# A transformer block on one core: 512-token chunks, contraction tiles of 128 and 64 rows, a clock warm-up and a planned order

## The chip, the cores and the metric

The kernel runs on one core of one Trainium2 chip. The metric is the device time of one execution in microseconds (us). An execution is called slow when it lies over 1.5% above the fastest of the same kernel; only fast runs are compared. TensorE (PE in the profile) does the matmuls, VectorE (DVE), ScalarE (ACT) and GpSimd (POOL) the rest, and SyncE (SP) issues the transfers.

## The reference

2048 tokens of width 448, 16 heads of 28, hidden width 1792; everything is bfloat16.

```python
mod = silu(c) @ w_mod                       # six vectors of 448: sa, ca, ga, sb, cb, gb
h = layernorm(x) * (1 + ca) + sa
q, k, v = split(h @ wqkv)                   # 16 heads of 28
# each token attends to itself and to the 7 tokens before it at distances 2, 4, ... 14
x = x + ga * (softmax(q k / sqrt(28)) v) @ wo
h = layernorm(x) * (1 + cb) + sb
x = x + gb * (silu(h @ w1) @ w2)
```

Since the window steps by 2, even and odd tokens ("parities") never meet in attention. Both kernels treat them as two sequences of 1024 and cut each into 9 blocks of 114 queries, each with 128 keys.

## The kernel before

The width 448 is contracted as 4 tiles of 112 rows. The parts that matter:

```python
KT, KP = 4, 112
x_view = A_x...rearrange("(a p two) d -> two a p d", two=2, p=128)   # one token per row: 896 bytes

def transposes(ts, ...):                    # one token tile: 4 transposes, 112 columns apart
    for j, t in enumerate(ts):
        for k in range(KT):
            T.transpose(ps[:, k, c0:c0 + 128], t[:, KP * k:KP * k + 128], ident[:])

def mod_cols(vecs, dst0):                   # modulation vectors as columns: 64 matmuls of one column in all
    for i, v in enumerate(vecs):
        for j in range(KT):
            for k in range(KT):
                T.matmul(ps[0:m, i, j:j + 1], lhsT=wmod[:, k, ...], rhs=scT[:, k:k + 1], ...)

def wo_unit(a):                             # output projection
    for kk in range(KT):
        T.matmul(ps[:, 0:D], lhsT=oT[par][:, kk, ...], rhs=wo[:, kk, :], ...)

# first FFN product: 1024 tokens of a parity as 384 + 384 + 256 columns
T.matmul(ps[:, j, 0:n], lhsT=w1[:, kk, ...], rhs=h2T[k % 2][:, kk, 0:n], ...)
# ... six groups of blocks; attention of group k+1 is woven with the FFN of group k, in program order
```

## Time and profile before

| | before |
|---|---|
| median time (first three runs) | 216.81 us (216.11 to 219.19) |
| profiled run, its span | 220.84 us, 219.0 us |
| mean granted clock of TensorE, profiled run | 0.953 |
| the same in most fast runs | 0.97 |

The profiled run is 0.8 to 2.2% slower than the three others, at a lower clock than fast runs. Its parts and waits can be read, but its span is some 0.017 x 219 = 4 us too long (an estimate from the two clocks).

TensorE's "busy" time overstates its work, because the ends of pipelined matmuls are modelled. For this document I therefore sum **occupancy**: from the start of each matmul to the start of the next, less the idle time that the trace marks between them, added up by the tile that is written. "At full clock" means the mean of those issued while the granted clock was 1.0, times their number. What the occupancy has above that I call the half-clock excess. These sums are worked out from the records of the traces and stand in no view as they are.

### The profile page before, as it was taken

To read this page: it belongs to the slowest core of one execution; us is meant where nothing else is said; L and a number is where in the kernel's file an instruction comes from. 1 tells how busy PE (TensorE), PEld (TensorE's weight loads), DVE (VectorE), ACT (ScalarE), POOL (GpSimd) and SP (SyncE) were. 2 spreads that over 40 slices of the span, in tenths; PEclk is the share of its full clock that TensorE was granted. 3 is DMA by queue.
4 is the path that set the end of the run, shared out by engine and by line. 5 is a ranking of instruction groups with operands and counts; after the bars stand their busy time and mean duration, and the time that the engine had idled before them with its cause. 6 is when DMAs were issued, how large, how long until landed. Compare 5 with 4: busy or idle time off the path is not lost.

```text
span 219.0 us, 4124 instructions
## 1 busy us (share of the span) xinstructions
PE 194.5 (89%) x1739; PEld 118.0 (54%) x1739; DVE 122.7 (56%) x274; ACT 102.2 (47%) x133; POOL 17.3 (8%) x55
## 2 busy tenths in 40 slices
PE   0157999499968999999999999999999999999990
PEld 0143556237735456554665546866475546555840
DVE  4176386927899355755453186773887457642011
ACT  3004449254172656474425767428753735430610
POOL 2802004000021000010001000001000100010000
PEclk9999999757995999999999999999999999999996
DMA  5999999300000000001000001000000010001001
GB/s 153 267 229 227 220 221 229 115 0 0 3 0 3 0 1 3 0 0 45 21 3 0 0 24 43 3 0 0 24 21 3 0 44 22 0 4 42 21 27 28
DMA packets 9072, 11.22 MB, mean 51 GB/s; under 512 B 472, under 2 KB 8152, under 8 KB 9048
## 3 DMA queue, kind: packets, MB, share of 16 engines
q1 hardware_dynamic: 9040, 10.90, 21.0%
q8 instruction: 15, 0.25, 0.5%
q14 instruction: 9, 0.07, 0.1%
q10 hardware_dynamic: 8, 0.00, 0.0%
HBM read 9.06 MB, written 1.84 MB: 50 GB/s over the span
## 4 chain that ended last, share of the span: by engine, by line
PE 75%; DMA 9%; DVE 7%; SPq 4%; POOL 2%; issue 1%
PE ps_h L395 22%; PE ps_y L411 20%; PE ps_qk L235 9%; DMA x_all<-in_A_x_dram 9%; PE ps_v L243 6%; PE ps_wo L350 5%; PE ps_l L265 4%; PE ps_o L330 3%; PE ps_t L195 3%; DVE st L174 2%; PE ps_ot L343 2%; POOL rs L177 1%; SPq L108 1%; DVE xn L449 1%; SPq L98 1%; DVE qk L237 1%
## 5 line engine op out<-in xcount | busy, mean ns | idle before, releaser
L395 PE MATMUL ps_h<-h2T,w 112*128 112x384 bf16 (+1 forms) x336 | 53.9, 308 | 0.0
L396 ACT ACTIVATE hid<-ps_h 128x768 bf16<-128x768 f32 (+1 forms) x42 | 31.0, 739 | 41.5 <-PE ps_h L395 41.4
L411 PE MATMUL ps_y<-w,hid 128*128 128x448 bf16 x224 | 46.3, 353 | 0.0
L395 PEld LDWEIGHTS <-w 112*128 112x128 bf16 x336 | 32.2, 98 | 15.8
L267 ACT ACTIVATE p<-ps_l 128x912 bf16<-128x912 f32 (+1 forms) x36 | 33.1, 934 | 15.5 <-PE ps_l L265 15.4
L235 PE MATMUL ps_qk<-h1T,wp 112*128 112x456 bf16 (+2 forms) x192 | 36.6, 340 | 1.1 <-DVE h1T L206 0.7
L411 PEld LDWEIGHTS <-hid 128*128 128x128 bf16 x224 | 20.1, 98 | 18.2
L302 DVE TENSOR_TENSOR p<-p,maskb 128x1824 bf16<-128x1824 bf16 (+1 forms) x18 | 19.8, 1103 | 13.6 <-ACT p L267 13.6
L235 PEld LDWEIGHTS <-wp 112*128 112x128 bf16 x192 | 19.2, 105 | 12.8 <-issue 6.1
L174 DVE BATCH_NORM_STATS2 st<-x_all 128x6 f32<-128x448 bf16 x32 | 19.2, 614 | 3.8 <-DMA x_all<-in_A_x_dram 3.4
L415 DVE TENSOR_TENSOR ot<-ps_y,x_all 128x448 bf16<-128x448 f32 x16 | 9.9, 622 | 19.5 <-PE ps_y L411 19.5
L243 PE MATMUL ps_v<-wqkv,h1T 112*128 112x448 bf16 x72 | 17.7, 389 | 0.0
L265 PE MATMUL ps_l<-qk 28*128 28x114 bf16 (+1 forms) x288 | 14.3, 219 | 3.6 <-DVE qk L237 2.8
L176 POOL TENSOR_TENSOR rs<-mv,epsb 128x2 f32<-128x2 f32 (+2 forms) x11 | 3.2, 293 | 173.6 <-DVE mv L175 173.6
L265 PEld LDWEIGHTS <-qk 28*128 28x128 bf16 x288 | 8.3, 96 | 16.0 <-issue 15.5
L206 DVE TENSOR_SCALAR h2T<-ps_t,modc 112x384 bf16<-112x384 bf16 (+1 forms) x24 | 9.4, 448 | 11.8 <-PE ps_t L195 11.8
L351 DVE TENSOR_TENSOR x_all<-ps_wo,x_all 128x448 bf16<-128x448 f32 x16 | 10.0, 624 | 10.2 <-PE ps_wo L350 10.2
L204 ACT ACTIVATE h1T<-ps_t,modc 112x512 bf16<-112x512 bf16 (+1 forms) x10 | 6.3, 688 | 20.0 <-DVE h1T L206 20.0
L245 ACT CAST v<-ps_v 128x448 bf16<-128x448 f32 x18 | 8.8, 535 | 14.6 <-PE ps_v L243 14.4
L195 PE MATMUL ps_t<-ident,xn 128*128 128x128 bf16 x128 | 12.2, 251 | 3.7 <-DVE xn L185 2.5
L350 PE MATMUL ps_wo<-wo,oT 112*128 112x448 bf16 x64 | 14.6, 353 | 0.0
L237 ACT CAST qk<-ps_qk 128x912 bf16<-128x912 f32 (+2 forms) x12 | 8.8, 731 | 10.5 <-PE ps_qk L235 10.5
(63 smaller groups left out, 155.7 us busy)
## 6 DMA issues: line engine op xcount, KB each, us to landing
w<-in_B_w_dram SPq DMA_DIRECT2D x2, 1568.0 KB, 23.3
out_dram<-ot SPq DMA_DIRECT2D x16, 112.0 KB, 1.7
wmod<-in_w_mod_dram SPq DMA_DIRECT2D x1, 1568.0 KB, 19.2
x_all<-in_A_x_dram SPq DMA_DIRECT2D x3, 448.0 KB, 18.3
wqkv<-in_A_wqkv_dram SPq DMA_DIRECT2D x3, 392.0 KB, 10.8
wmod<-in_w_mod_dram SPq DMA_DIRECT2D x1, 784.0 KB, 8.4
x_all<-in_A_x_dram SPq DMA_DIRECT2D x2, 224.0 KB, 2.9
wo<-in_A_wo_dram SPq DMA_DIRECT2D x1, 392.0 KB
```

The lines of the kernel that those rows point to most:

```text
L174: V.bn_stats(out=st[:, j, :], in_=x_all[:, u, :])
L195: T.transpose(ps[:, k, c0:c0 + 128], t[:, KP * k:KP * k + 128], ident[:])
L235: T.matmul(ps[:, j, 0:n], lhsT=wp[:, k, 16 * typ + 4 * g:16 * typ + 4 * g + 4, :].rearrange("p h d -> p (h d)"), rhs=h1T[par][:, k, HALO + ...
L237: (S.copy if on_act else V.tensor_copy)(out=dst, in_=ps[:, :, 0:n])
L243: T.matmul(ps[:, j, 0:D], lhsT=h1T[par][:, k, BQ * b + 2:BQ * b + 130], rhs=wqkv[:, k, 2 * D:3 * D], start=(k == 0), stop=(k == KT - 1))
L265: T.matmul(ps[:, j, g * nq:(g + 1) * nq], lhsT=qk[par][r:r + DH, 4 + g, BQ * b + 2:BQ * b + 130], rhs=qk[par][r:r + DH, g, HALO + BQ * b:H ...
L267: S.activation(out=pbuf(par, b)[:, t, :, :, 0:nq], in_=ps[:, :, 0:4 * nq].rearrange("p j (g q) -> p j g q", q=nq), func=ACTF.Exp, scale=SCALE)
L302: V.tensor_tensor(out=p, in0=p, in1=maskb[:, 1 if b == 0 else 0, 0:nq].unsqueeze(1).to_broadcast([128, H, nq]), op=ALU.mult)
L350: T.matmul(ps[:, 0:D], lhsT=oT[par][:, kk, 128 * a:128 * a + 128], rhs=wo[:, kk, :], start=(kk == 0), stop=(kk == KT - 1))
L395: T.matmul(ps[:, j, 0:n], lhsT=w1[:, kk, 128 * f:128 * f + 128], rhs=h2T[k % 2][:, kk, 0:n], start=(kk == 0), stop=(kk == KT - 1))
L396: S.activation(out=hid[k % 2][:, 2 * i:2 * i + 2, 0:n], in_=ps[:, :, 0:n], func=ACTF.Silu)
L411: T.matmul(ps[:, 0:D], lhsT=hid[k % 2][:, f, 128 * j:128 * j + 128], rhs=w2[:, f, :], start=(f == 0), stop=(f == NF - 1))
```

## The change

The intent: wider matmuls (512 columns instead of 342 to 456), loads with longer rows on all 128 partitions, a warm TensorE clock at the first projection, no table switches between exponential and Silu, and no holes, by running all attention ahead of the FFN in an order that a list scheduler plans on the host. The diff, cut to its core:

```diff
-KT, KP = 4, 112
+KT, K3 = 4, D - 384                        # contraction 448 = 3 x 128 + 64
+NC, CP = 4, 256                            # 4 chunks of 512 consecutive tokens: 256 of each parity
+WARM, LA = 26, 3                           # LA: how many chunks attention runs ahead of the FFN
+def half(j):
+    return slice(K3 * j, K3 * j + K3)      # rows 0 to 63 or 64 to 127
+def rows_of(k, j=0):
+    return half(j) if k == 3 else slice(0, 128)

-x_view = ...rearrange("(a p two) d -> two a p d", two=2, p=128)
+x_view = ...rearrange("(c i p t) d -> c p i (t d)", c=NC, i=2, t=2)    # two tokens per row: 1792 bytes

 # transposes of a token tile, for both norms (and the same five for the attention output)
-    for k in range(KT):
-        T.transpose(ps[:, k, c0:c0 + 128], t[:, KP * k:KP * k + 128], ident[:])
+    for k in range(3):
+        T.transpose(ps[:, k, ...], x[:, 128 * k:128 * k + 128], ident[:])
+    for h in range(2):                     # the last 64 columns go to both halves of the rows
+        T.transpose(ps[half(h), 3, ...], x[:, 384:D], ident[:])

 # modulation columns
-        T.matmul(ps[0:m, i, j:j + 1], lhsT=wmod[:, k, ...], rhs=scT[:, k:k + 1], ...)
+        for h in range(1 + (j == 3)):
+            T.matmul(ps[rows_of(j, h), i, j:j + 1], lhsT=wmod[rows_of(k), k, ...], rhs=scT[rows_of(k), k:k + 1], ...)

 # output projection
-    T.matmul(ps[:, 0:D], lhsT=oT[par][:, kk, ...], rhs=wo[:, kk, :], ...)
+    T.matmul(ps[:, 0:D], lhsT=oT[rows_of(kk), kk, par, ...], rhs=wo[rows_of(kk), kk, :], ...)

 # Q, K and the first FFN product, in pairs of pairs: 6 full, 4 half, 6 full matmuls of 512 columns
+def duo(mms, ...):
+    for j in range(2):
+        for k in range(3):
+            mms[0](p0, j, k, k == 0, False)
+    for j in range(2):
+        mms[0](p0, j, 3, False, True)      # 64 rows each: product j on half j of the array
+    for j in range(2):
+        mms[1](p1, j, 3, True, False)
+    for j in range(2):
+        for k in range(3):
+            mms[1](p1, j, k, False, k == 2)

+def warm_up(o):                            # 27 times, while the weights load
+    T.matmul(warm[0][:, 0, :], lhsT=ident[:], rhs=ident[:].unsqueeze(1).to_broadcast([128, 4, 128]), ...)

-weave(...)                                 # hand-made order
+class Plan: ...                            # list scheduler with a cost in ns for every operation, for example
+    P.op(("pe", 280.0), tr, ...)           #   five norm transposes
+    P.op(("pe", 250.0), tr, ...)           #   five transposes of the attention output
+    P.op(("pe", 756.0), wo_mm, ...)        #   output projection of one token tile
```

## The prediction

> **What bounds the kernel now.** I read the page's busy line first, then the busy time by stretches, then TensorE's waits, then the chain in order of time. The page:
>
> ```profile
> PE 194.5 (89%) x1739; PEld 118.0 (54%) x1739; DVE 122.7 (56%) x274; ACT 102.2 (47%) x133; POOL 17.3 (8%) x55
> ```
>
> TensorE leads, but busy is not useful here. I cut the span where its behaviour changes (columns: busy us and instruction count of each engine, granted clock, DMA share, GB/s):
>
> ```profile
> 0.00:16.16 16.16, 3.68 (x49) 3.35 (x50) 7.02 (x35) 2.01 (x4) 6.65 (x37) 1.00 0.91 216
> 16.16:24.30 8.14, 6.98 (x29) 3.35 (x29) 5.04 (x15) 2.73 (x6) 1.20 (x2) 1.00 1.05 221
> 24.30:39.30 15.00, 15.00 (x136) 8.46 (x135) 9.26 (x27) 10.53 (x15) 2.42 (x4) 1.00 1.08 234
> 39.30:42.10 2.80, 0.01 (x1) 0.03 (x1) 2.80 (x4) 0.00 (x0) 0.00 (x0) 0.90 0.32 102
> 42.10:51.70 9.60, 9.56 (x55) 4.18 (x55) 3.99 (x4) 5.59 (x8) 0.00 (x0) 0.50 0.01 2
> 51.70:75.00 23.30, 20.67 (x242) 13.84 (x240) 18.92 (x42) 9.73 (x14) 2.12 (x2) 0.85 0.01 1
> 75.00:213.60 138.60, 138.58 (x1233) 84.75 (x1231) 75.04 (x150) 71.60 (x89) 4.91 (x10) 1.00 0.04 14
> 213.60:219.00 5.40, 0.00 (x0) 0.00 (x0) 0.62 (x1) 0.00 (x0) 0.00 (x0) 0.68 0.10 29
> ```
>
> From 75 us on TensorE is never free and never slowed, and VectorE and ScalarE are half idle: that stage is bound by TensorE. Before 75 us it is idle for 19.1 us (12.5 of them before its first projection at 16.16) and slow twice at a granted clock near one half. There is a third slow stretch that the clock column hides: between 18.2 and 24.3 us the weight loads of the 456-column projections follow each other at 0.38 us, which is 456 columns at 1.2 per ns, half pace; after 24.3 us at 0.19. What TensorE waited for, and what its groups cost once warm (waits; then pieces of the chain: start, us, matmuls):
>
> ```profile
> PE ps_m L215 <- DMA wmod<-in_w_mod_dram: 7.0, 1, 7.0
> PE ps_l L265 <- DVE qk L237: 2.8, 1, 2.8
> PE ps_t L195 <- DVE xn L185: 2.5, 2, 1.7
> ```
> ```profile
> 75.80 1.65 PE ps_qk L235 x8
> 77.45 1.51 PE ps_v L243 x8
> 80.89 1.30 PE ps_h L395 x8
> 88.26 0.76 PE ps_wo L350 x4
> 208.29 5.31 PE ps_y L411 x28
> ```
>
> The first wait is the start (weights not there), the second is the hole at 39 to 42 us after which the clock drops. Eight 384-column matmuls take 1.30 us, 162 ns each; 448 columns take 189 ns.
>
> **What the Trainium skill says.** (1) "TensorE: Matmul & The Clock Gate", Part 1: the array starts at 1.2 GHz, is released to 2.4 after a busy window of about 3.4 us and throttled after an idle one. The trace agrees on the halving (0.50 from 42.1 to 51.7) but the fall follows a hole of 2.8 us and the return took over 9 us of busy work, so recovery costs more here than the page's window. (2) Same page, "Back-to-back issue gap": N/2.4 + 2.5 ns. Agrees: 160 + 2.5 for 384 columns. (3) Same page, Part 3: matmuls in different row groups run at once. The logits of before use row groups of 32: eight 114-column matmuls, 50 ns each alone, take 0.30 us from their start to the next group's (75.43 to 75.73 in the timeline), so 0.75 of the serial time and not half. (4) "DMA: Bandwidth & Descriptors", Measured: 341 GB/s for a transfer of 1 MB. The loads of before reach it only at the end:
>
> ```profile
> 9.00:15.00 6.00, 3.01 (x46) 2.93 (x47) 2.92 (x11) 0.00 (x0) 2.28 (x17) 1.00 1.13 227
> 27.00:34.00 7.00, 7.00 (x78) 4.02 (x75) 5.36 (x12) 3.66 (x6) 0.99 (x2) 1.00 1.04 214
> 37.00:39.00 2.00, 2.00 (x22) 1.20 (x19) 0.60 (x3) 1.76 (x2) 1.21 (x2) 1.00 1.09 307
> ```
>
> At 27 to 34 us the first FFN weight moves with rows of 3584 bytes on 112 partitions, at 37 to 39 the second with rows of 896 bytes on 128. So long rows alone don't speed a load in this trace; filling 128 partitions may.
>
> **The change, part by part.**
> *Contraction 448 as 3 x 128 + 64 instead of 4 x 112.* The 64-row remainders of two products sit on two halves of the array, so eight passes become six full and two half ones. With the 0.75 from the logits a pair of 512-column outputs costs 6 x 0.216 + 2 x 0.75 x 0.216 = 1.62 us. First FFN product: 28 x 1.62 = 45.4 us, against 224 x 0.1625 + 112 x 0.109 = 48.6. Q and K: 16 x 1.62 = 25.9 against 27.8. V: 9 x (6 + 1.5) x 0.189 = 12.8 against 13.6. Together 5.9 less. Wider matmuls as such give only 2.5 ns for each one saved, already in these sums. Unchanged: second FFN product 224 x 0.190 = 42.5, output projection 64 x 0.19 = 12.1, logits 36 x 0.30 = 10.7, attention times V 18 x 0.405 = 7.3. Dearer: five transposes instead of four for each token tile, 9.0 against 7.9 for the norms and 4.5 against 3.7 for attention; modulation columns 80 x 36 ns = 2.9 against 2.35. Gates 1.5. Sum: **174.6 us of TensorE work, against some 180** before (138.6 after 75 us, 41.6 before it).
> *Clock warm-up.* 27 dummy matmuls of 512 columns in the time when TensorE waits for weights anyway. They cost nothing and can save the half-speed stretch 16.2 to 24.3: 6.98 busy at half pace, 3.5 us.
> *Start.* The first projection needs tokens (0.46 MB), modulation weights (0.80) and now the whole QKV weight (1.20): 2.46 MB; before, 2.06 without V. In before the QK weight landed some 0.85 MB of traffic after its own bytes. From 2.1 us at 225 GB/s that would be 15 us plus 1 us for the padding copies: no gain. At 290, a choice of mine between the two rates above, with the lag halved: 2.1 + 2.9/0.29 = 12.1, plus 1: first projection at about **13 us**.
> *Attention ahead of the FFN, planned order.* It removes the holes at 35 to 45 and 60 to 70 us and, with them, the slow stretches: 5.4 idle and up to 4.8 + 3.1 of lost clock. Table loads go from 11 to about 3, 1.28 us each on ScalarE, none on the path. But the phase without FFN then has about 81 us of TensorE work against: VectorE fixed 66 (statistics of 16 tiles x 0.73 = 11.7, normalize 5.4, masks 18 x 1.05 = 18.9, division 14.2, residual 9.3, gating and rest 6.5), ScalarE fixed 33 (36 exponentials at 0.857 back to back = 30.9, a table load or two), and 44 to 46 of copies that either may do. 145 over two engines is 72 each, 89% of TensorE's 81. Chains through four engines in a static order won't fill that: I allow **7 us** of holes. The FFN phase has 92 us of TensorE against 26 on ScalarE (28 Silu of 0.93) and 33 on VectorE: no holes.
> *Sum.* TensorE work 174.6 less the 2.7 that falls ahead of the first projection (one modulation, first transposes) = 171.9; start 13; holes 7; a stall for late gates or weights 0 to 2, say 1; tail as now 5.4: 198.3 of span. A run's time is 1.84 above its span (220.84 against 219.0): 200.1. I shade it to **198.5**, because the planner's costs agree with this trace (table load 1290 against 1283 ns, half passes 0.72 against my 0.75) and its loads are set at over 300 GB/s, so its author may have seen faster ones.
>
> **The rivals.**
> *Loads no faster.* For it: 214 to 230 GB/s with long rows. The order is fixed by planned landing times, so an in-order TensorE that meets a gate before its weights came stalls, and the warm-up ends early and the clock falls back. First projection at 16, 3 us of cold work, 4 us of stall: 206 to 210.
> *Attention phase bound by ScalarE and VectorE.* For it: 89% load on both, three large PSUM buffers, five probability buffers, no FFN work as filler; holes near 3 us make the clock drop for 9. Against it: projections of later chunks fill. Holes of 15 and one drop of 5: 208 to 213.
> *Row halves run fully together or not at all.* Fully: FFN, QK and V save another 0.25 x 2 x 0.216 x 53 = 5.7: 193. Not at all, or each change of tiling drains the array: 204 to 207.
> *All as planned.* Start 11.5, holes 2, no stall: 190 to 192.
>
> **Range and chances.** The terms that I chose, start (11.5 to 16), holes (2 to 15) and pairing (-5.7 to +6), are nearly independent and give about 9 us either way: 189 to 208. Same within 2% means over 212.5, which needs two rivals at once: 0.06; slower needs all and a repeated clock drop: 0.02; faster 0.92.
>
> **What would show it.** Right: first projection of Q and K at about 13 us at 0.22 us for each 512-column matmul; DMA of 270 GB/s or more in the first 20 us; eight passes of a FFN pair in about 1.62 us; TensorE idle about 7 us between the first projection and the last exponential, none after; no clock under 0.9 after 13 us; tail about 5.4. Wrong: a wait of TensorE on a weight load of over 3 us, attention-phase waits on masks or exponentials above 12 us in sum, pairs at 1.75 us or more.

## The result, and the profile after

The changed kernel is **slower**: 228.94 us median (227.83 to 230.01, four runs, all fast) against 217.19 for the kernel before in the same rounds. The ratio is 1.053, with an interval of 1.044 to 1.062. Ratios here are the mean time of one kernel's fast runs over that of the other's of the same rounds, so they are not quite the ratio of the medians quoted. The profiled run took 230.01 us, with a span of 227.9 us and a mean granted clock of 0.922.

First the page: busy time, and the granted clock in 40 slices of the span, in tenths (the fives are slices wholly at half clock).

```profile
PE 210.9 (93%) x1656; PEld 99.3 (44%) x1656; DVE 111.6 (49%) x245; ACT 102.9 (45%) x125; POOL 20.2 (9%) x60
...
PEclk9979995579999999995559999999999999999998
```

TensorE has become busier, from 194.5 to 210.9 us, though the change was to take work from it. Next, busy time by stretches, cut where the behaviour changes (same columns as in the prediction: busy us and count of PE, PEld, DVE, ACT, POOL; granted clock, DMA share, GB/s).

```profile
0.00:16.01 16.01, 13.55 (x89) 7.11 (x89) 6.37 (x26) 1.75 (x3) 5.27 (x32) 0.89 0.91 318
...
35.15:48.80 13.65, 12.13 (x123) 6.07 (x123) 9.34 (x19) 7.08 (x10) 0.11 (x1) 0.50 0.01 2
48.80:99.50 50.70, 49.56 (x561) 23.88 (x559) 33.87 (x67) 35.97 (x46) 3.43 (x6) 1.00 0.01 1
99.50:104.83 5.33, 0.97 (x30) 0.70 (x24) 5.26 (x11) 3.00 (x4) 2.40 (x2) 0.87 0.00 0
104.83:120.48 15.65, 15.53 (x170) 8.60 (x170) 9.87 (x20) 8.59 (x12) 0.00 (x0) 0.50 0.01 2
120.48:222.50 102.02, 100.23 (x559) 44.24 (x555) 28.98 (x62) 31.90 (x33) 3.54 (x8) 1.00 0.05 17
```

Loads are fast now (318 GB/s up to the first projection), yet that projection starts at 16.0 us. There are still two long stretches at half clock while TensorE works, one of them after a hole at 99.5 to 104.8 us in which VectorE is busy for 5.26 of 5.33 us. From 48.8 to 99.5 us and again from 120.5 to 222.5 TensorE is busy for 98% of the time. So most of the lost time is in how long its work takes. The list of TensorE's waits has one long entry (tile, releaser, us in total, times, longest), and it is that hole:

```profile
PE ps_ot L636 <- DVE o L630: 4.4, 1, 4.4
```

Now the pieces of TensorE's work, from the timeline of the kernel after (start, us, matmuls of one group). Busy times overlap, so read from one start to the next.

```profile
7.88 2.86 PE L375 MATMUL ps_m<-scT,both 128*128 128x1 bf16 x40
...
137.23 1.03 PE L659 MATMUL ps_wo<-wo,oT 128*128 128x448 bf16 x4
138.19 1.04 PE L681 MATMUL ps_h<-h,w 128*128 128x512 bf16 x4
...
146.52 0.34 PE L424 MATMUL ps_t<-ident,xn 128*128 128x128 bf16 x3
146.79 0.25 PE L426 MATMUL ps_t<-ident,xn 128*64 128x128 bf16 x2
146.97 1.47 PE L681 MATMUL ps_h<-h,w 128*128 128x512 bf16 x6
...
158.77 1.46 PE L681 MATMUL ps_h<-h,w 128*128 128x512 bf16 x6
160.16 0.61 PE L683 MATMUL ps_h<-h,w 64*128 64x512 bf16 x4
160.70 1.47 PE L681 MATMUL ps_h<-h,w 128*128 128x512 bf16 x6
162.00 2.81 PE L705 MATMUL ps_y<-w,both 128*128 128x448 bf16 x14
```

The same groups in the timeline of the kernel before:

```profile
33.05 1.17 PE L215 MATMUL ps_m<-scT,wmod 112*128 112x1 bf16 x32
...
109.49 0.36 PE L343 MATMUL ps_ot<-ident,o 114*128 114x114 bf16 x4
109.69 1.33 PE L235 MATMUL ps_qk<-h1T,wp 112*128 112x342 bf16 x8
...
112.35 0.92 PE L350 MATMUL ps_wo<-wo,oT 112*128 112x448 bf16 x4
113.11 0.31 PE L235 MATMUL ps_qk<-h1T,wp 112*128 112x342 bf16 x1
```

A pair of pairs takes 162.00 - 158.77 = 3.23 us, 1.62 a pair: the predicted number, though not for the predicted reason (see "Why the prediction was wrong"). But the output projection of one tile takes 0.96 us instead of 0.76, though the columns and the count are the same. Five norm transposes take 0.45 us, 90 ns each, where 64 ns was the mean of one before. Forty one-column matmuls take 2.8 us to the start of the next group, 70 ns each, where 32 of before took at most 1.17, 37 each. What these dearer groups have in common is that they mix full matmuls (128 x 128) with some that use 64 rows or 64 columns.

The sums by tile, in us of occupancy at full clock:

| tile (work) | predicted | before | after |
|---|---|---|---|
| ps_h, ps_qk (first FFN product, Q and K) | 71.3 | 76.6 | 72.1 |
| ps_v | 12.8 | 13.9 | 14.1 |
| ps_y, ps_l, ps_o, ps_g (as before) | 62.0 | 64.2 | 62.7 |
| ps_wo (output projection) | 12.1 | 12.2 | 15.4 |
| ps_t (norm transposes) | 9.0 | 8.2 | 14.4 |
| ps_ot (attention transposes) | 4.5 | 3.6 | 7.7 |
| ps_m (modulation columns) | 2.9 | 2.1 | 5.5 |
| two small ones | 0 | 0.4 | 0.2 |
| **TensorE work** | **174.6** | **181.2** | **192.2** |
| warm-up dummies | 0 | 0 | 6.2 |
| half-clock excess | 0 | 13.3 | 12.6 |
| idle between matmuls | see the sum | 16.1 | 10.2 |
| until the first matmul; tail | see the sum | 3.0; 5.4 | 1.4; 5.4 |
| span | 196.7 | 219.0 | 227.9 |

The columns of the two traces add up to their spans but for rounding. (The prediction's span is its 198.5 less the 1.84 that it puts between span and run.) The work went up by 11.0 us. The holes that the new order removed (5.9) and the earlier first matmul (1.6) are a little more than the dummies fill (6.2). The half-clock excess is about the same in the two traces, but the trace before is a slow run: by the estimate above some 4 us of its 13.3 belong to the slow state, so a fast run would have about 9, and some 3 us of the loss may be a larger excess in the changed kernel. No fast run of the kernel before has a trace, so this split is not measured. The spans differ by 8.9 us and the medians by 11.8; by the same estimate the rest is the slow state of the profile before.

### The profile page after: what moved, and what is told of

Same layout as the page of the kernel before. It is cut to its first block, busy times and chain, and to the rows that moved or that the text cites. A ratio compares the mean times of both kernels' runs of the same rounds, so it can differ in the third digit from the quotient of the medians.

```text
span 227.9 us, 3929 instructions
## 1 busy us (share of the span) xinstructions
PE 210.9 (93%) x1656; PEld 99.3 (44%) x1656; DVE 111.6 (49%) x245; ACT 102.9 (45%) x125; POOL 20.2 (9%) x60
## 3 DMA queue, kind: packets, MB, share of 16 engines
q1 hardware_dynamic: 7824, 10.95, 14.5%
HBM read 9.12 MB, written 1.84 MB: 48 GB/s over the span
## 4 chain that ended last, share of the span: by engine, by line
PE 80%; DVE 9%; ACT 4%; issue 2%; DMA 1%; ACTq 0%; DVEq 0%
PE ps_y L705 19%; PE ps_h L681 17%; PE ps_qk L513 10%; PE ps_v L536 6%; PE ps_wo L659 5%; PE ps_t L424 4%; PE ps_l L566 3%; PE ps_h L683 3%; PE ps_o L623 3%; PE ps_m L375 3%; PE ps_t L426 2%; ACT p L574 2%; PE ps_ot L636 2%; DVE st L409 2%; ACT h L433 2%
## 5 line engine op out<-in xcount | busy, mean ns | idle before, releaser
L687 ACT ACTIVATE both<-ps_h 128x1024 bf16<-128x1024 f32 x28 | 28.5, 1024 | 47.6 <-PE ps_y L705 21.6
L705 PE MATMUL ps_y<-w,both 128*128 128x448 bf16 x224 | 44.4, 353 | 0.7 <-DVE ot L710 0.7
L681 PE MATMUL ps_h<-h,w 128*128 128x512 bf16 x168 | 41.8, 389 | 0.0
L574 ACT ACTIVATE p<-ps_l 128x912 bf16<-128x912 f32 (+1 forms) x36 | 31.6, 939 | 11.3 <-PE ps_l L566 11.2
L705 PEld LDWEIGHTS <-both 128*128 128x128 bf16 x224 | 21.4, 98 | 21.7 <-issue 2.1
L513 PE MATMUL ps_qk<-h,wp 128*128 128x512 bf16 (+1 forms) x128 | 28.9, 399 | 0.0
L681 PEld LDWEIGHTS <-w 128*128 128x128 bf16 x168 | 15.2, 99 | 19.8 <-issue 4.6
L433 ACT ACTIVATE h<-ps_t,modc 128x512 bf16<-128x512 bf16 x18 | 13.0, 776 | 18.3 <-DVE h L435 13.3
L409 DVE BATCH_NORM_STATS2 st<-x_all 128x6 f32<-128x448 bf16 x32 | 19.7, 615 | 3.2 <-DMA x_all<-in_A_x_dram 2.8
L517 ACT CAST qk<-ps_qk 128x1024 bf16<-128x1024 f32 x14 | 14.2, 1013 | 11.6 <-PE ps_qk L513 11.6
L659 PE MATMUL ps_wo<-wo,oT 128*128 128x448 bf16 x64 | 16.4, 356 | 0.0
L513 PEld LDWEIGHTS <-wp 128*128 128x128 bf16 (+1 forms) x128 | 9.3, 98 | 15.7 <-issue 8.1
L536 PE MATMUL ps_v<-wqkv,h 128*128 128x448 bf16 (+1 forms) x72 | 15.9, 379 | 0.1
L662 DVE TENSOR_TENSOR x_all<-ps_wo,x_all 128x448 bf16<-128x448 f32 x16 | 9.9, 617 | 11.0 <-PE ps_wo L659 10.9
## 6 DMA issues: line engine op xcount, KB each, us to landing
w<-in_B_w_dram SPq DMA_DIRECT2D x1, 1344.0 KB, 14.4
```

The source lines that it names most:

```text
L409: V.bn_stats(out=st[:], in_=x_all[:, us[j], :])
L433: S.activation(out=out_, in_=in_, func=ACTF.Identity, scale=scale, bias=shift)
L513: T.matmul(ps[:, j, :], lhsT=w.rearrange("p h d -> p (h d)"), rhs=h[rows_of(kk, j), kk, :, 128:128 + CP], start=start, stop=stop)
L536: T.matmul(ps[:, par, 0:D], lhsT=h[rows_of(kk, par), kk, par, b0:b0 + 128], rhs=w, start=(kk == 0), stop=(kk == KT - 1))
L574: S.activation(out=out_, in_=ps[:, :, 0:4 * nq].rearrange("p j (g q) -> p j g q", q=nq), func=ACTF.Exp, scale=SCALE)
L659: T.matmul(box["ps"][:, 0:D], lhsT=oT[rows_of(kk), kk, par, s0:s0 + 128], rhs=wo[rows_of(kk), kk, :], start=(kk == 0), stop=(kk == KT - 1))
```

## The experiments

**My theory after the result (A):** each change between full tiles (128 x 128) and 64-row or 64-column tiles costs TensorE about 0.1 us, and the small groups, which change twice for a handful of short matmuls, lose more by it than the pairs win. The Trainium skill has the mechanism, which I had not applied to these groups: "TensorEngine Tiling (Array Packing)", Key Properties, says that changing the tiling mode drains the engine. It states no duration. The traces show the lost time at each change, not what the array does in it. **Rivals:** the fixed order makes the time, and holes and slow stretches grow wherever the work shrinks (B); the clock is lost because of certain groups (C); the lead of attention over the FFN makes the hole and the half clock (D); the warm-up costs or earns something (E); the order is bad because the planner's costs are stale (F); short matmuls do not count as busy for the clock (G); they can keep a full clock but not win back a lost one (H). The letters return in the expectations.

### 1 to 4. The dear groups with full tiles

`t_full` (only the norm transposes; the last 64 columns are normalized twice, so that four full transposes fill both halves):

```diff
-xn = [ct([128, D], ...)]
+xn = [ct([128, 512], ...)]
+V.tensor_scalar(out=t[:, D:512], in0=x_all[:, us[j], 384:D], ...)      # a second normalization of 64 columns
-for k in range(3): T.transpose(...)
-for h in range(2): T.transpose(box["ps"][half(h), 3, ...], box[j][:, 384:D], ident[:])
+for k in range(KT): T.transpose(box["ps"][:, k, ...], box[j][:, 128 * k:128 * k + 128], ident[:])
```

> The changed kernel with one edit: the two 64-column transposes of each token tile in the norms become one full 128-column transpose (the normalized tile carries its last 64 columns twice); order of all else kept. In the trace of the changed kernel 160 transposes take 89.9 ns each from start to start at the full clock, 14.4 us; 128 took 64.4 ns in the kernel before, 8.2 us. Theory A (each change of the tile shape costs TensorE time, and that is what eats the gain): transposes fall to about 8.2 us, time falls by about 6 us, to 223. Rival B (the fixed order makes the time: TensorE has holes and half-clock stretches wherever its work is shorter): transposes shorter but time within 2 us of 228.9.

Measured: two fast runs (221.54 and 219.91 us) and two slow ones, median 222.49; the two fast ones over the mean of the six fast runs of before (216.75) give 1.018, without an interval. Occupancy of ps_t fell from 14.4 to 7.7 us. The time fell by some 8 us, more than that, since the half-clock excess of this run was about 3 us smaller too.

`o_full` (attention transposes and output projection; zeros fill the other 64 rows):

```diff
-ob = [ct([128, D], ...)]
+ob = [ct([128, 512], ...)]                                             # columns 448 to 511 zeroed once
+V.memset(wo[half(1), 3, :], 0.0)
-three full and two 64-column transposes
+for kk in range(KT): T.transpose(box["t"][:, kk, 0:nq], box["o"][0:nq, 128 * kk:128 * kk + 128], ...)
-T.matmul(..., lhsT=oT[rows_of(kk), kk, ...], rhs=wo[rows_of(kk), kk, :], ...)
+T.matmul(..., lhsT=oT[:, kk, ...], rhs=wo[:, kk, :], ...)
```

> The changed kernel with one edit: attention output padded with zeros to 512 columns, so that its transposes and the output projection use full tiles only. In the changed kernel these took 7.7 us and 15.4 us of TensorE at full clock, in the kernel before 3.6 and 12.2. Theory A: about 4.0 and 12.2, time down by about 7 us, to 222. Rival B: time within 2 us of 228.9.

Measured: 223.27 us, ratio 1.023 (1.013 to 1.032). ps_wo 15.4 to 12.9 us, ps_ot 7.7 to 4.7.

`m_full` (modulation columns and gates, zeros again; column tile 3 reads columns 320 to 447 so that it is full, and two tiny copies bring its upper half down):

```diff
+V.memset(wmod[half(1), 3, :], 0.0)
-for h in range(1 + (j == 3)): for k in range(KT): T.matmul(ps[rows_of(j, h), ...], lhsT=wmod[rows_of(k), k, ...], ...)
+for k in range(KT): T.matmul(ps[:, i, j:j + 1], lhsT=wmod[:, k, c0:c0 + 128], rhs=scT[:, k:k + 1], ...)
```

> The changed kernel with one edit: the modulation columns as 64 full-tile matmuls instead of 80 of four shapes, and full-tile gates. TensorE work 5.5 to about 2.4 us and 1.9 to 1.5. Theory A: time down 3.5 us from that alone. Theory C (the clock falls when a window of about 3.4 us holds only tiny matmuls, and the two modulation blocks of 2.8 and 3.0 us are such windows): the half-clock stretches that start at 11.3 and 35.1 us vanish or shrink, another 1.5 to 8 us. If C is wrong both stretches stay, and the time falls by 3.5 at most, to 225.

Measured: 223.07 us, ratio 1.021 (1.012 to 1.031); the profiled run was slow. ps_m fell from 5.5 to 1.7 us. The half-clock stretches moved (34.7 to 38.1, 72.2 to 79.1 and 96.1 to 116.6 us instead of 11.3 to 14.7, 35.2 to 48.8 and 103.4 to 120.5), but their sum stayed: excess 13.3 against 12.6. The early drop at 11 us is also gone in t_full, which has the old columns, and is present in o_full. So theory C isn't confirmed; it stays open, because one-column matmuls by themselves did lose the clock in the probe below. The time gained (some 3%) is larger than the 3.8 us of columns, but with an interval of one per cent either way and another clock pattern I read no more into it.

`all_full` (all three edits):

> The three edits together, order kept. Theory A: TensorE work down by about 16.5 us at the full clock; if it is the bound, time 228.9 - 16.5 = 212, and less (to 204) if the half-clock stretches at 11 and 35 us go too. Rival B: holes and half-clock stretches grow to take the place, time above 220.

Measured: **212.54 us** (211.61 to 213.41), ratio **0.979** (0.972 to 0.986): faster than both kernels, though the interval does not place it clearly beyond 2%. The work fell from 198.3 (with dummies) to 182.0 us of occupancy, 16.3 less; the median time is 16.4 less than that of the changed kernel. That the two agree so closely is partly luck: idle time rose from 10.2 to 14.2 us while the excess fell from 12.6 to 8.2. Two groups in its timeline:

```profile
17.43 0.72 PE L429 MATMUL ps_t<-ident,xn 128*128 128x128 bf16 x8
...
84.02 0.93 PE L660 MATMUL ps_wo<-wo,oT 128*128 128x448 bf16 x4
```

Eight transposes, two token tiles, take 0.72 us with their modelled end, where two tiles of five took 0.90 without it. The projection came down from 1.03 to 0.93, both with modelled ends; before had 0.92. This settles theory A in the kernel itself: the shape of a few small groups turns about 5% slower into 2% faster, and rival B, which expected over 220 us, falls. The edits also remove matmuls (160 to 128, 90 to 72 and 80 to 64), but the two narrow transposes of a group run at the same time (see the probe), so fewer transposes save no pass, and 16 columns of 25 ns are only 0.4 us (an estimate). On VectorE the edits add work.

What is left in all_full is a hole and a stretch at half clock after it, in its stretches (same columns as above):

```profile
33.86:40.69 6.83, 6.04 (x56) 2.98 (x57) 5.38 (x9) 3.77 (x6) 0.00 (x0) 0.50 0.00 0
...
90.82:96.49 5.67, 0.38 (x11) 0.21 (x9) 5.60 (x12) 2.22 (x3) 2.41 (x2) 0.59 0.00 0
96.49:105.54 9.05, 8.79 (x139) 7.80 (x140) 7.79 (x19) 4.63 (x6) 0.00 (x0) 0.50 0.01 2
```

In the hole VectorE works 5.60 of 5.67 us: it normalizes for the first FFN chunk and masks probabilities, in order, while TensorE waits for a division that stands behind them. Idle is 14.2 us in sum and the half-clock excess 8.2.

### 5, 6 and 10. The warm-up

`no_warm` keeps the changed kernel's order and only leaves the dummies out:

```diff
 def warm_up(o):
+    return
```

> The changed kernel without its 27 dummy matmuls, order of all else kept. Theory E (the warm-up earns its place): the clock is at half from the start until dense projections have run for a while, as in the kernel before (full from 24.4 us); about 10 us of work at half pace cost 5, less the 1.7 us by which the dummies delay the first transposes: time 2 to 4 us longer, 231 to 233. Rival: the clock at 16 us depends on the work just before, not on the dummies, which only stand in the way: 227 to 229.

Measured: 229.08 us median of four; its two fast runs took 227.28 and 227.01, ratio 1.040 (1.030 to 1.050); the changed kernel has 1.053. In its profiled run, a slow one, the clock is full only from 19.7 us on instead of 14.7, and the run time does not grow by it. Theory E (that the warm-up is worth a few us here) falls.

`before_warm` adds 27 such dummies to the start of the kernel before:

```diff
+ps_w = big.tile([128, 2, 512], F32, ...)
+for _ in range(27):
+    T.matmul(ps_w[:, 0, :], lhsT=ident[:], rhs=ident[:].unsqueeze(1).to_broadcast([128, 4, 128]), ...)
 st0 = stats([0, 1])
```

> The kernel before with one part of the change alone: the same 27 dummy matmuls at its start. If they hold the clock up to the first projection at 16.2 us, the half-pace stretch to 24.4 us goes, 3.5 us: 213.5. If the clock falls again during the tiny matmuls and waits from 10 to 16 us, nothing is gained: 217 within 1.

Measured: 221.5 us, ratio 1.016 (1.009 to 1.024). It says nothing of the dummies: with them, the automatic order put the late modulation columns ahead of the first projection, where TensorE waited 9.5 us for their weights, and the clock was half from 13.3 to 30.4 us. Inconclusive.

`all_nowarm` is all_full without dummies, by the same one-line edit:

> As all_full (0.979 of the kernel before) without the 27 dummy matmuls, order kept. In the changed kernel itself leaving them out cost nothing (1.040 against 1.053 of the kernel before). With full tiles the dummies end right before the first projections (clock full from 6.6 to 33.9 us in all_full), so here they should earn something: 0.985 to 0.995. Rival: they earn nothing here either: 0.970 to 0.980.

Measured: 213.73 us, ratio 0.987 (0.979 to 0.994); all_full had 0.979. That lies in the range expected if the dummies earn something, but the difference of 0.8% is between two calls and the intervals overlap: whether they earn anything here is not shown.

### 7, 8 and 11. The planned order

`all_replan` is all_full with some twenty planner costs set to measured ones, for example:

```diff
-P.op(("pe", 1406.0), vmm, ...)             # V of one block
+P.op(("pe", 1550.0), vmm, ...)
-P.op(("dve", 335.0), norm, ...)
+P.op(("dve", 480.0), norm, ...)
```

> Full tiles for all small work as in all_full (212.5 us), and the planner's costs set to what the traces show (V 1550 ns, attention times V 440, logits 300, residual 590, copies and modulation a tenth dearer), so the order is a new one. Theory F (an order planned on wrong costs makes the holes): idle time of TensorE between its matmuls falls from 14.2 us to under 9 and with the hole near 95 us its half-clock stretch: 204 to 207. Rival: holes come from the attention stage as such, the time stays at 211 to 214 in a different order.

Measured: 213.92 us, ratio 0.977 (0.969 to 0.986). The order is another one and the longest hole shrank to 2.9 us, but idle is 14.5 us and the excess 10.2 (its profiled run was slow, which may enlarge the excess). Same time; theory F falls.

`all_la1` and `all_la2` are all_full with attention at most one, or two, chunks ahead of the FFN:

```diff
-LA = 3
+LA = 1        # all_la2: 2
```

> As all_full (212.5 us), but attention runs one chunk ahead of the FFN instead of three (one constant), so that FFN matmuls lie between attention work, at the price of more table loads on ScalarE, 1.28 us each. Theory D (a long stage of attention without dense matmuls is what costs the clock and the holes: 8.2 us of half-clock excess and 14.2 us idle in all_full): excess under 4, idle under 10: 203 to 207. Rival: table loads and the wrong costs make as many holes: 211 to 216.

> As all_full with attention two chunks ahead instead of three. If where the FFN lies doesn't matter, as all_la1 said (0.979 with one chunk ahead): 0.97 to 0.99. If a mixed order is better than both ends: under 0.965.

Measured: all_la1 213.45 us, ratio 0.979 (0.972 to 0.985), idle 13.2, excess 7.1. all_la2 214.02 us, ratio 0.990 (0.981 to 1.000), idle 16.3, excess 8.8. Theory D falls: the lead is worth nothing measurable in either direction.

### 9 and 12. Small matmuls by themselves

`probe` is no block but a row of stages on TensorE, with 60 dense 512-column matmuls ahead of each (its output is zeros but for a few columns). Its output is wrong, which doesn't matter for the time. It and probe2 ran once each. Cut:

```python
for i in range(240): T.transpose(pt[...], w[:, ...], ident[:])                    # full
for i in range(40):                                                               # as in the change
    for k in range(3): T.transpose(pt[:, ...], w[:, 128 * k:128 * k + 128], ident[:])
    for h in range(2): T.transpose(pt[64 * h:64 * h + 64, ...], w[:, 384:448], ident[:])
# ... 420 of 28 rows and 114 columns; 560 of 29 columns; 560 of one column; 240 of 128 columns
# ... 16 groups of 448 columns: 3 of 128 rows and one of 64
```

> A kernel of TensorE work alone, wrong in its result on purpose: stretches of some 14 us of one kind of small matmul each, without any wait, between stretches of 60 dense 512-column matmuls. In order: full transposes; transposes three full and two of 64 columns, as in the norms of the changed kernel; 28-row 114-column matmuls on alternating row groups, as the logits; 29-column matmuls; one-column matmuls; full 128-column matmuls; and 448-column groups of three full and one of 64 rows, as the output projection. Theory A: the mixed transposes take 0.45 us for five at the full clock (90 ns each), the full ones 60 ns each; the mixed 448-column groups 0.96 us, against 0.76 for four full ones. Theory G (the clock counts only the array's work, not the engine's busy time): the granted clock falls to 0.5 within two windows of 3.4 us in the stretches of transposes, logits, 29- and one-column matmuls, although TensorE is busy throughout, and comes back a window or two after dense work begins. Rival: busy without a gap keeps it at 1.0 in all of them, and only waits lose it.

Its timeline, the full transposes and one group of five:

```profile
18.19 13.56 PE L47 MATMUL p_tr<-ident,w 128*128 128x128 bf16 x240
...
44.80 0.25 PE L53 MATMUL p_tr<-ident,w 128*64 128x128 bf16 x2
44.98 0.34 PE L51 MATMUL p_tr<-ident,w 128*128 128x128 bf16 x3
45.25 0.25 PE L53 MATMUL p_tr<-ident,w 128*64 128x128 bf16 x2
```

Full ones take 13.56 / 240 = 56.5 ns each. A mixed five takes 45.25 - 44.80 = 0.45 us, 90 ns each, just as in the changed kernel, with no wait on any other engine in the way. In the records the two narrow transposes start 4 ns apart (44.803 and 44.807 us): they run at the same time, so a mixed five is four passes of 56.5 ns, 0.226 us, and two changes of shape, 0.22 us, **0.11 each**. (If the five ran one after the other, 0.285 us, 0.08 each would be left.) A group of three 448-column matmuls and one of 64 rows takes 0.97 us, again as in the changed kernel (0.96); four full ones at 189 ns are 0.76, so two changes cost 0.21, 0.10 each. A matmul of 29 columns takes 25.8 ns and one of a single column 25.0, in full tiles.

The clock stayed at 1.0 through the transposes, the 28-row matmuls (10.9 us of them) and the 29-column ones. Only the one-column matmuls lost it, 5.3 us after they began (the expectation of probe2 says 7), with TensorE busy all the time:

```profile
136.00:140.00 4.00, 4.00 (x155) 4.00 (x152) 0.00 (x0) 0.00 (x0) 0.50 0.01 4
```

So theory G is right for one column and wrong for the rest.

`probe2` turns the question round: lose the clock with 480 one-column matmuls, then see what brings it back.

```python
dense(60); tiny(480)
for i in range(220): T.transpose(...)                                              # full
dense(60); tiny(480)
for i in range(500): T.matmul(ph[i % 2][:, 0:114], lhsT=w[32 * (i % 2):..., 0:128], rhs=...)   # 28 rows
# ... the same with 600 of 29 columns, then with 8 of 28 rows and 4 of 448 columns in turn
```

> A second kernel of TensorE work alone, wrong in its result on purpose. Four times: 60 dense 512-column matmuls, then 480 one-column matmuls (12 us, in which the first probe lost the clock after some 7 us), then one kind of work for 13 us or so: full transposes; logits-like 28-row matmuls; 29-column matmuls; alternating groups of eight logits and four 448-column matmuls. Question: which work brings a lost clock back. Theory H (what keeps the clock is not enough to win it back): with transposes, logits and 29-column matmuls the clock stays at 0.5 through their whole stretch and returns only in the dense one after it, as in the changed kernel from 103 to 120 us; with the mixed groups it returns in one to three windows of 3.4 us. Rival: any work that kept the clock in the first probe brings it back within one or two windows, so the long half-clock stretches of the changed kernel come from its waits.

```profile
32.20:35.76 3.56, 3.56 (x36) 3.56 (x35) 0.00 (x0) 0.00 (x0) 0.50 0.00 0
35.76:46.00 10.24, 10.24 (x186) 10.24 (x184) 0.00 (x0) 0.00 (x0) 1.00 0.01 3
...
71.80:95.60 23.80, 23.80 (x501) 23.64 (x500) 0.00 (x0) 0.00 (x0) 0.50 0.01 3
```

The transposes, which start at 32.0, have the full clock back after 3.7 us; the 29-column matmuls after 3.5. The 28-row ones, shaped like the logits, ran for 24 us, busy without a gap, and never got it back. Eight of them in turn with four of 448 columns took 8.8 us. So theory H holds for logits alone: they keep a full clock and do not regain a lost one. In the changed kernel TensorE is busy from 104.8 us with logits, attention times V and mixed transposes, and the clock stays half until 120.5, which is 3.5 us after the first 512-column matmuls (117.0 us). That fits, but the mixture wasn't taken apart, so it is consistent and not shown.

### 13 and 14. The hole

In `all_mf6` and `all_mf67` the statistics of the FFN norms wait until the masks of block 6 (of blocks 6 and 7) are done, so that VectorE serves attention first:

```diff
-st = [P.op(("dve", 730.0), ..., [src[us[i]]]) ...]
+st = [P.op(("dve", 730.0), ..., [src[us[i]]] + list(late)) ...]     # late = [masked[b, q] for b in (6,) for q in range(2)]
```

> As all_full (0.979 of the kernel before; hole of 5.3 us near 91 us, then half clock to 105 us), but the statistics of the first FFN norm wait until the masks of block 6 (first of the last chunk) are done; the planner makes a new order with that. If VectorE's order makes that hole and the hole loses the clock: no wait of TensorE above 3 us near there, half-clock excess from 8.2 to about 3, time 0.94 to 0.96. Rival: the wait and the clock loss appear elsewhere in the attention stage, time 0.97 to 0.99.

> The same with the masks of blocks 6 and 7. Same two outcomes: 0.94 to 0.965 if the order was the cause (a little later statistics may cost up to 2 us at the start of the FFN), 0.97 to 0.99 if the loss only moves.

Measured: 215.19 us, 0.990 (0.984 to 0.997), longest wait 4.8 us, idle 16.1, excess 7.9; and 215.67 us, 0.994 (0.987 to 1.000), longest wait 4.3, idle 17.1, excess 7.0. The hole only moves, and both are rather slower than all_full (0.979, in another call); all_mf67 lies above both expected ranges. What order, or which buffers, would fill it stays **open**: idle of 13 to 17 us and an excess of 7 to 10 are in every variant of all_full.

## Why the prediction was wrong

It said 198.5 us, 189 to 208, faster with 0.92. Measured: 228.94, slower by 5%. By its own steps:

- **Bound by TensorE: right.** It still sets the pace, and from 120.5 us on, mostly FFN, it is idle for only 1.8 of 102 us. That is why added TensorE work came through to the time: 16.3 less work, 16.4 less time, the close match being partly luck (see all_full).
- **The pairs: the number right, by luck.** 1.62 us a pair predicted and measured, but as half passes that overlap in part, at 0.75 of a pass each. In the records two half passes start 4 ns apart (160.162 and 160.166 us): they overlap wholly. The rest is the change of shape: six full passes take 160.16 - 158.77 = 1.39 us when half passes follow, and 162.00 - 160.70 = 1.30 when full ones follow. Four half passes take the time of two full ones, 0.43, and two changes some 0.2; that this is about the 4 x 0.75 x 0.216 = 0.65 of the prediction is chance. The 0.75 came from misreading the logits of before:

```profile
75.43 0.37 PE L265 MATMUL ps_l<-qk 28*128 28x114 bf16 x8
75.73 1.71 PE L235 MATMUL ps_qk<-h1T,wp 112*128 112x456 bf16 x8
```

  The eight start two by two, 3 or 4 ns apart, 49 to 60 ns from pair to pair, and the next group starts 0.14 us after the last two instead of 0.05. So the 0.30 us was half the serial time and 0.1 us for a change of shape: the cost that sank the prediction stood in the trace before. For V (7.5 passes of 189 ns) the number was wrong too: 12.8 predicted, 14.1 measured, 195 ns for each of eight matmuls, because there only two half passes share two changes, and together they cost as much as two full passes.
- **"Dearer: five transposes instead of four ... 9.0 ... and 4.5", "modulation columns 80 x 36 ns = 2.9", output projection "Unchanged: ... 12.1": this is the step that failed.** They measured 14.4, 7.7, 5.5 and 15.4: 14.5 of the 17.6 us by which the work (192.2 against 174.6) missed. I multiplied a new number of matmuls by the old time of one, although the new ones have another shape beside full ones. As an estimate: 100 changes of shape in the two kinds of transposes (two in each of 50 groups of five), 32 in the output projections and 40 in the columns, 0.1 us each, are 17.2 us, less some 2.7 because the two narrow transposes of a group run together: about 14.5. The rival "each change of tiling drains the array: 204 to 207" named the mechanism, but sized it only for the pairs of half passes and not for the small groups.
- **"Holes ... and, with them, the slow stretches": wrong in the second half.** Holes of 7 us and a stall of 1 were predicted; idle is 10.2 in all. But the half-clock excess, predicted as none, is 12.6, at least as much as before (13.3 in a slow run, some 9 by the estimate for a fast one). This is the second failed term. It explains in the main why the gain stayed away; what makes the kernel slower is mostly the 11.0 us of added work.
- **Start at 13 us: wrong by 3 to 5, though its rate was on the safe side.** QKV weights landed 7.2 us after their issue, and 318 GB/s flowed where 290 was assumed. The first projection came at 16.0 (V) and 17.9 (Q and K), because 40 mixed modulation columns took 2.86 us, five dummies stood behind them, and twenty mixed transposes ran at half clock from 12.25 to 14.9. In all_full V starts at 12.2 us, with the dummies still there, so the cause is in the main the same failed step. Two slips in the working: the 15 us at 225 GB/s already has the halved lag (with all of it 2.1 + 3.3/0.225 = 16.8 us), and the loads of before did not reach 341 GB/s at the end but 307.
- **Warm-up: "can save ... 3.5 us": not shown.** Without it the changed kernel is no slower, and all_full by 0.8%, with intervals that overlap.
- **Tail 5.4: right. Table loads 11 to 3: right,** and none is on the path.
- **The last shading was a false comfort.** I trusted the planner because two of its costs agreed with the trace. Its own span for the changed order, computed afterwards by its own code, is 198.7 us, the same as my number: it has 280, 250 and 756 ns where the trace has 450, 428 (7.7 / 18) and 965. Two counts that share an assumption do not confirm each other.

The three terms of the range were start, holes and pairing. None was the cost of the small groups, so the range could not hold it.

## What to carry to other kernels

When a contraction doesn't divide by 128, look at what the remainder tile does to the short groups: here each change between full and 64-wide tiles cost 0.10 to 0.11 us, more than a whole 128-column matmul (57 ns), so pad the small groups with zeros to full tiles. Half tiles paid only where four long half passes shared two changes (3.23 us for a pair of pairs, against 16 x 0.216 = 3.45 in full passes); with two half passes, in V, they did not (1.56 against 8 x 0.189 = 1.51). When a group takes longer than its passes, look at where its matmuls start before calling the rest a partial overlap. Price an operation of a new shape by measuring it among its neighbours, not by its count times the old mean, and above all when a planner uses the same costs. A hole can cost more than its length: after the one of 4.4 us TensorE worked for 15.7 us at half clock. In probe2 the kind of matmul decided how long the half clock lasted (3.5 us to over 24); in the kernel that was not taken apart.

## What the Trainium skill lacked or had wrong

- "TensorEngine Tiling (Array Packing)", Key Properties: it says that a change of mode drains the engine, but not what that costs. Here it was 0.11 us a change in the probe's transposes (0.45 us for four passes of 56.5 ns and two changes) and 0.10 in the output projection (0.96 against 0.76 us with two changes).
- "TensorE: Matmul & The Clock Gate", Part 4, says that transposes do not count as busy for the clock and that the full clock doesn't engage for them. Here 13.6 us of nothing but transposes kept it at 1.0, and transposes alone brought a lost one back in 3.7 us.
- The same page, Part 1, has one rule for a warm clock, a busy window of about 3.4 us. Here 28-row matmuls kept a full clock for 10.9 us but did not regain a lost one in 24 us of unbroken work, and one-column matmuls lost a full one after 5.3 us though TensorE was never idle (one run each). No page has these two.
